# Nine slots of the first three experts: plain loads in place of gathers in a two-stage FFT and expert kernel

## The chip, the cores and the metric

The kernel runs on one core of a Trainium2 chip. The metric is the device time of one execution in microseconds (us); lower is better. The engines are named as the profile names them: PE (TensorE, with PEld for its weight loads), DVE (VectorE), ACT (ScalarE), POOL (GpSimd) and SP (SyncE, which here only issues DMAs). The times shown are those of three runs; one further execution was profiled.

## The reference

The input `x` has 8 batches of 1856 rows of 256 numbers. The real part of its two-dimensional Fourier transform per batch gives 14,848 tokens of 256 features. Each token goes to one of 16 experts (4 groups of 4), and each expert is a two-layer network.

```
X = np.fft.fft(np.fft.fft(x, axis=1), axis=2).real      # 8 x 1856 x 256 -> tokens
g_idx = argmax(tokens @ w_group)                        # group
e_idx = argmax(tokens @ w_expert[g_idx])                # expert in the group
h = relu(token @ w1[g_idx, e_idx])                      # 256 -> 1024
out[token] = g_weight * e_weight * (h @ w2[g_idx, e_idx])  # 1024 -> 256
```

## The kernel before

Phase 1 (`phase1`) goes through the eight batches: it folds the rows, multiplies with cosine and sine tables, picks an expert for each token (`route`) and scatters the tokens, 260 words each, into a table `XS` in DRAM. There each expert owns 122 x 128 rows. A block of 128 rows is a slot, and seven slots of each expert (`NSLOT`) are static, which means that they are always computed. Rows beyond them are handled in overflow slots. The scatters are indirect DMAs on POOL's queue, 14 or 15 per batch. The order of work in phase 1 is written out by hand in the strings `ORDER0` to `ORDER8`.

Phase 2 (`phase2`) is a list of jobs. Jobs 0, 1 and 2 are the first four slots of experts 0, 1 and 2. They are "early": their rows are all there after an early batch, or are left as they were filled. Jobs 3, 4 and 5 are the remaining three static slots of experts 0, 1 and 2 (together the nine slots of the change). From job 6 on, each further expert has a job of four slots, one of three and one overflow slot. A scheduler in the compiler sets the order of the instructions on each engine where the code does not pin it.

A job needs its rows `xg` in SBUF. `turn_steps` makes of each slot a high half (`xh`, an ACT cast) and a low half (`xh`, a DVE subtraction), and a DMA transpose on SP's queue writes both to `xT`. Layer 1 (`layer1`) takes 8 blocks of hidden units, 6 matmuls `ph` each. ACT and DVE then write `hT` from `ph`. There are four `ph` buffers (`UB`), so block 4 waits for the `hT` of block 0. Layer 2 (`layer2`) takes 24 matmuls `py` per slot, an ACT step that writes `y`, and a scatter to `out` on POOL. The weights of each expert come in four parts (`wst`, 512 KB each, on SP's queue).

The rows of a static slot come by an indirect DMA on POOL's queue (`gather`). Its indices `ii` lie outside the table for rows beyond the expert's count, so these rows of the buffer stay as they were. There are eight `xg` buffers (`XGB`), all set to 1 at the beginning. The rows of an early slot come by plain DMAs on SP's queue (`early_load`). For that reason the twelve early slots of `XS` are filled with ones at the beginning, in the first pass over the batches, so that no row of them is undefined.

Of the kernel before, what the change touches and what calls it, by code (L numbers as in the profile page):

```python
# [10 lines left out]
F32 = mybir.dt.float32  # L11
F16 = mybir.dt.float16
I32 = mybir.dt.int32
# [9 lines left out]
P = 128  # L23
# [7 lines left out]
CAP = ROWS * P  # L31
RWID = 260
NSLOT = 7
# [66 lines left out]
def earliest():  # L100

    return {e: n for _, w in waves() for e, _, n in w}
# [156 lines left out]
def bc(ap, axis, n):  # L259

    a = ap.unsqueeze(axis)
    shape = list(a.shape)
    shape[axis] = n
    return a.broadcast_to(shape)


class K:
# [538 lines left out]
    def phase1(self):  # L806
        tc, nc, cp, ps = self.tc, self.nc, self.cp, self.ps
        self.late, rows = ExitStack(), ExitStack()
        xp, ub, rp = (s.enter_context(tc.tile_pool(name=n, bufs=k, side="right"))
                      for s, n, k in ((self.late, "xq", 4), (self.late, "ub", 1), (rows, "row", 1)))  # L810
        with tc.tile_pool(name="ua", bufs=1) as ua, tc.tile_pool(name="fft", bufs=1) as fp:
            self.fp = fp
            self.misc = ps.tile([P, 512], F32, name="misc", tag="misc")
            self.load_small()
            xs = {0: self.load_x(0, xp, 2)}
            self.CS = fp.tile([P, 2, 2, 4, NK], F16, name="CS")
            cs = self.ap["cs"].rearrange("p (t h c k) -> p t h c k", t=2, h=2, c=4)
            for tr in range(2):
                for c in range(4):
                    nc.sync.dma_start(out=self.CS[:, tr, :, c], in_=cs[:, tr, :, c])  # L820
                if tr == 0:
                    nc.sync.dma_start(out=self.c16, in_=self.ap["c16"])
                    xs[1] = self.load_x(1, xp)
            self.rt = self.wp.tile([P, 4096], F32, name="wst")[:, 0:512]
            nc.sync.dma_start(out=self.rt, in_=self.ap["c32"][:, C_RT:])
            nc.sync.dma_start(out=self.c32[:, C_LATE:], in_=self.ap["c32"][:, C_LATE:C_RT])
            self.carry = self.c32[:, C_OFF:C_OFF + NE]
            self.ex = [cp.tile([P, NCM, 2, 5], F32, name=f"ex{i}") for i in range(2)]
            for ex in self.ex:
                nc.gpsimd.memset(ex, 1e-9)  # L830
            whl = self.wpa.tile([P, 2, 4096], F16, name="whl").rearrange("p h n -> p (h n)").bitcast(F32)
            self.rowts = [whl[:, 0:NC * RWID].rearrange("p (n d) -> p n d", d=RWID),
                          rp.tile([P, NCM, RWID], F32, name="row")]
            self.rowt = {}
            for t in self.rowts:
                nc.gpsimd.memset(t[:, :, D + 2:RWID], 0.0)
            for i in range(XGB):
                xg = self.xp2.tile([P, RWID], F32, name="xg")
                nc.gpsimd.memset(xg, 1.0)

            def run(gens, order, rest=True, keep="N"):

                for _ in self.run(gens, order):
                    pass
                for k, g in gens.items():
                    if rest and g and k not in keep:
                        for _ in g:
                            pass

            self.queues = {k: [] for k in "sIidlt"}  # L850
            self.fds, Us = {}, {}
            self.open = self.parts = 0
            self.first = {"G": self.fold(0, xs.pop(0), fp), "H": self.nyquist_in()}
            run(self.first, START, False)
            F, W, X, Z = self.fold(1, xs.pop(1), fp), None, None, None
            for b in range(B):
                g = {"Z": Z, "F": F}
                F = None
                if b + 2 < B:
                    xs[b + 2] = self.load_x(b + 2, xp)  # L860
                    F = self.fold(b + 2, xs.pop(b + 2), fp)
                g["N"] = F
                if b == 0:
                    for e, n in earliest().items():
                        self.Q.dma_start(out=self.XS[e * CAP:e * CAP + n * P].rearrange("(s p) c -> p s c", p=P),
                                         in_=bc(xg[:, :].bitcast(I32), 1, n))
                if b == W0_AT:
                    self.st0 = self.wp.tile([P, 4096], F32, name="wst")
                    for i in range(8):
                        s = slice(i * 512, i * 512 + 512)  # L870
                        self.later("t", lambda s=s: tc.keep_in_program_order(
                            nc.sync.dma_start(out=self.st0[:, s], in_=self.ap["w12"][0, :, s])))
                Us[b] = (ua, ub)[b % 2].tile([P, 2, 2, NK], F16, name="U")
                g["S"] = self.s_stage(b, Us[b])
                g["U"] = self.nyquist_rows(b, Us[b], ub)
                if b == 0:
                    g.update(self.first)
                    g["Y"] = self.first["Y"] = self.nyquist()
                    g["R"] = self.router_weights()
                else:  # L880
                    g.update(self.rows_of(b - 1, Us.pop(b - 1), xp))
                if b == 5:
                    W, X = self.first_weights(), self.first_turn()
                g["W"], g["X"] = W, X
                Z = g["R"] if 0 < b < LASTZ else None
                run(g, {0: ORDER0, 5: ORDER5, 6: ORDER6, 7: ORDER7}.get(b, ORDER),
                    keep="N" + ("R" if Z else "") + ("WX" if b < B - 1 else ""))
            self.last = self.rows_of(B - 1, Us.pop(B - 1), xp)
            rows.close()
# [51 lines left out]
    def early_load(self, e, r, Q):  # L941

        xg = self.xp2.tile([P, RWID], F32, name="xg")
        o = e * CAP + r * P
        self.of_batch(Q.dma_start(out=xg[:, :].bitcast(I32), in_=self.XS[o:o + P, :]).ins, self.early[e, r][0])
        return xg

    def of_batch(self, ins, b):
# [219 lines left out]
    def phase2(self, wp):  # L1168
        tc, nc = self.tc, self.nc
        wpa = self.wpa  # L1170
        with tc.tile_pool(name="h", bufs=2, reuse_waits="tile") as hp, \
# [10 lines left out]
            first = earliest()  # L1182
# [7 lines left out]
            for e in range(len(first), NE):  # L1190
# [3 lines left out]
                o = e - len(first)  # L1194
# [17 lines left out]
            st, ready, infos, xs = {}, {0: self.w0}, {}, {}  # L1212
# [3 lines left out]
            def tail():  # L1216
                if state["tail"]:
                    try:
                        next(state["tail"])
                    except StopIteration:  # L1220
                        state["tail"] = None
                        pool["wo"] = later.enter_context(
                            tc.tile_pool(name="wo", bufs=1, side="right", reuse_waits="tile"))
# [32 lines left out]
            def fetch(n):  # L1256
                if n >= len(jobs):
                    return
                _, kind, slots = jobs[n]
                if kind != "e" and not infos:  # L1260
                    while state["tail"]:
                        tail()
                    infos["s"] = self.static_info()
                    infos["o"] = self.overflow_info()
                if kind == "e":
                    if n >= len(self.x0):
                        xs[n] = [self.early_load(*j, nc.sync) for j in slots], [self.early[j][1] for j in slots]
                else:
                    ii, ge = infos[kind]
                    xs[n] = ([self.gather(self.xp2, ii[:, j:j + 1]) for j in slots],  # L1270
                             [ge[:, j:j + 1] for j in slots])

            def prep(n):
# [13 lines left out]

            pend = None
            fetch(0)
            finish(prep(0))  # L1290
            fetch(1)
            loads()
            for n, (u, kind, slots) in enumerate(jobs):
# [69 lines left out]
```

## Time and profile before

| what | value |
|---|---|
| median of three runs | 862.84 us (862.5 to 863.77) |
| profiled execution, own time | 861.9 us |
| its span, first to last instruction | 860.1 us |
| PE busy | 807.9 us (94%) |
| ACT, DVE, POOL busy | 579.1, 533.5, 385.1 us |
| mean granted TensorE clock | 0.985 of full speed |
| gathers of static slots | 100, 106.8 us of POOL |

The table is read from the busy shares of the page. PE is the engine with the largest share, so a stage in which PE stands still is where time can be gained or lost.

### The profile page before, as it was taken

How to read it: one execution, taken by the hardware profiler on the slowest of the kernel's cores; microseconds unless marked ns; L12 is line 12 of the kernel's file. 1: busy time of each engine (PE TensorE's matmuls, PEld its weight loads, DVE VectorE, ACT ScalarE, POOL GpSimd, SP SyncE). 2: the span in 40 equal slices, each digit the busy share in tenths (PEclk: the TensorE clock that was granted, in tenths of full speed). 3: DMA queues.
4: the chain of work that ended last, by engine and by line, in shares of the span. 5: the costliest groups of instructions: out<-in, count | busy, mean ns of one | idle time of the engine just before them, and what ended most of it. 6: DMA issues, size and time to landing. Idle time of an engine off the chain costs nothing.

```text
span 860.1 us, 17724 instructions
## 1 busy us (share of the span) xinstructions
PE 807.9 (94%) x6375; PEld 578.8 (67%) x6375; DVE 533.5 (62%) x1346; ACT 579.1 (67%) x1190; POOL 385.1 (45%) x372
## 2 busy tenths in 40 slices
PE   2789899969979999999999999999999999999997
PEld 0457666647547767676768686868686868686866
DVE  6499989666736456474838474747475656654440
ACT  2477667776738578595959687777677776866441
POOL 1007777776876425334434343435252526240303
PEclk9999999979989999999999999999999999999999
DMA  9914663585697545465756465757474848261201
GB/s 347 356 65 172 220 229 120 179 241 150 209 295 152 182 149 178 150 172 161 182 163 190 154 190 149 209 133 222 123 231 111 255 87 271 69 170 40 57 10 42
DMA packets 110186, 145.89 MB, mean 170 GB/s; under 512 B 76395, under 2 KB 81799, under 8 KB 108304
## 3 DMA queue, kind: packets, MB, share of 16 engines
q1 hardware_dynamic: 92768, 99.96, 38.9%
q0 software_dynamic: 16896, 44.55, 17.4%
q8 instruction: 51, 0.84, 0.4%
q14 instruction: 39, 0.32, 0.1%
q10 hardware_dynamic: 432, 0.22, 0.1%
HBM read 97.18 MB, written 33.29 MB: 152 GB/s over the span
## 4 chain that ended last, share of the span: by engine, by line
PE 56%; issue 6%; ACT 4%; DMA 4%; DVE 2%; POOL 1%; POOLq 0%; SPq 0%; ACTq 0%; DVEq 0%
PE ph L1129 28%; PE py L1145 28%; DMA xT<-xh 2%; ACT junk L245 2%; ACT whl L245 1%; POOL out L797 1%; DMA wst<-w 1%; ACT hT L1132 1%; DVE hT L1133 1%; DMA xg<-XS,ii_s 1%; DVE whl L245 1%; ACT y L1150 0%; ACT xh L1090 0%; DVE xh L1092 0%; DVE e_v L245 0%
## 5 line engine op out<-in xcount | busy, mean ns | idle before, releaser
L1129 PE MATMUL ph<-xT,whl 128*128 128x512 f16 (+2 forms) x2112 | 355.5, 318 | 13.0 <-DVE hT L1133 6.0
L1145 PE MATMUL py<-whl,hT 128*128 128x256 f16 x2976 | 354.2, 273 | 0.7 <-ACT y L1150 0.5
L1145 PEld LDWEIGHTS <-hT 128*128 128x128 f16 x2976 | 288.5, 98 | 55.7 <-issue 1.2
L1133 DVE SCALAR_TENSOR_TENSOR hT<-ph,hT 128x512 f16<-128x512 f32 (+2 forms) x352 | 179.6, 529 | 151.3 <-ACT hT L1132 149.5
L1129 PEld LDWEIGHTS <-whl 128*128 128x128 f16 x2112 | 182.3, 98 | 133.7 <-issue 16.5
L797 POOL DMA_INDIRECT out<-y,tok x124 | 136.7, 1102 | 267.9 <-ACT y L1150 238.9
L1132 ACT ACTIVATE hT<-ph 128x512 f16<-128x512 f32 (+2 forms) x352 | 157.0, 473 | 64.3 <-PE ph L1129 62.0
L1076 POOL DMA_INDIRECT xg<-XS,ii_s x100 | 106.8, 1068 | 99.0 <-ACT xh L1090 43.7
L245 DVE SCALAR_TENSOR_TENSOR whl<-wst,e_v,whl 128x1024 f16<-128x1024 f32 x112 | 137.8, 1281 | 19.8 <-ACT whl L245 19.6
L245 ACT ACTIVATE whl<-wst,e_v 128x1024 f16<-128x1024 f32 x112 | 120.9, 1139 | 14.5 <-DVE e_v L245 12.8
L245 ACT ACTIVATE junk<-wst 128x1024 bf16<-128x1024 f32 x112 | 119.1, 1063 | 7.7 <-DMA wst<-w 7.7
L1150 ACT ACTIVATE y<-py,cws 128x256 f32<-128x256 f32 x124 | 58.3, 471 | 69.5 <-PE py L1145 64.8
L1092 DVE TENSOR_TENSOR xh<-xg,xh 128x256 f16<-128x256 f32 x112 | 46.5, 419 | 87.3 <-ACT xh L1090 87.2
L245 PE MATMUL pu<-CS,ghl 128*128 128x464 f16 (+3 forms) x384 | 83.9, 369 | 4.6 <-ACT ghl L245 4.6
L797 POOL DMA_INDIRECT XS<-whl,posi x42 | 44.9, 1070 | 74.6 <-ACT row L245 62.3
L1090 ACT CAST xh<-xg 128x256 f16<-128x256 f32 x112 | 42.8, 402 | 50.7 <-DMA xT<-xh 40.4
L245 PEld LDWEIGHTS <-ghl 128*128 128x128 f16 (+1 forms) x384 | 44.3, 119 | 35.9 <-ACT ghl L245 4.9
L797 POOL DMA_INDIRECT XS<-row,posi x45 | 50.2, 1116 | 14.0 <-issue 11.6
L245 PEld LDWEIGHTS <-U 128*128 128x128 f16 x672 | 44.3, 99 | 12.9 <-issue 5.4
L245 PE MATMUL pr<-c,U 128*128 128x256 f16 x336 | 47.6, 279 | 3.4 <-ACT row L245 2.5
L245 DVE TENSOR_TENSOR xq<-xq 128x514 f32<-128x514 f32 x64 | 41.1, 685 | 6.4 <-DMA xq<-xq 6.3
L245 ACT CAST U<-pu 128x464 f16<-128x464 f32 (+3 forms) x64 | 33.2, 549 | 9.2 <-PE pu L245 8.9
(150 smaller groups left out, 429.7 us busy)
## 6 DMA issues: line engine op xcount, KB each, us to landing
wst<-w SPq DMA_DIRECT2D x108, 512.0 KB
xq<-xq SPq DMA_DIRECT2D x14, 1028.0 KB
CS<-cs SPq DMA_DIRECT2D x8, 464.5 KB
xq<-xq SPq DMA_DIRECT2D x4, 514.0 KB
wst<-w SPq DMA_DIRECT2D x8, 256.0 KB
xT<-xh SPq DMA_TRANSPOSE x124
out<-y,tok POOLq DMA_INDIRECT x124, 4.0
xg<-XS,ii_s POOLq DMA_INDIRECT x100, 6.4
```

Of the source, the lines that this page charges most:

```text
L245: return self.tc.keep_in_program_order(f(*args, **kw))
L797: ins = self.nc.gpsimd.indirect_dma_start(out=out, out_offset=bass.IndirectOffsetOnAxis(ap=ap, axis=0), in_=in_, in_offset=None, bounds_ch ...
L1076: self.nc.gpsimd.indirect_dma_start(out=xg[:, :].bitcast(I32), out_offset=None, in_=self.XS[:, :], in_offset=bass.IndirectOffsetOnAxis(ap= ...
L1090: A.copy(xh[:, 0], xg[:, 0:D])
L1092: lo = V.tensor_tensor(out=xh[:, 1], in0=xg[:, 0:D], in1=xh[:, 0], op=ALU.subtract)
L1129: nc.tensor.matmul(ph[:, 0:n * P], lhsT=w[:, wl, o:o + P], rhs=xT[:, xl * 2 + c, :], start=i == 0, stop=i == 5)
L1132: nc.scalar.activation(hT[:, f, 0], ph[:, 0:n * P], AF.Relu)
L1133: nc.vector.scalar_tensor_tensor(out=hT[:, f, 1], in0=ph[:, 0:n * P], scalar=0.0, in1=hT[:, f, 0], op0=ALU.max, op1=ALU.subtract)
L1145: nc.tensor.matmul(py, lhsT=hT[:, f, hl, j * P:(j + 1) * P], rhs=w[:, wl, 2048 + f * D:2048 + (f + 1) * D], start=i == 0, stop=i == 23)
L1150: nc.scalar.activation(y, py, AF.Copy, scale=cw)
```

## The change

`XS` is filled with ones in two steps: the early slots 0 to 3 of experts 0, 1 and 2 in the pass of batch 0, as before, and their slots 4 to 6 in the pass of batch 1. The nine slots are then read with `row_load`, a plain DMA of 128 rows on SP's queue, and no longer with `gather` on POOL's queue.

```diff
-                if b == 0:
+                if b < 2:
                     for e, n in earliest().items():
-                        self.Q.dma_start(out=self.XS[e * CAP:e * CAP + n * P].rearrange("(s p) c -> p s c", p=P),
-                                         in_=bc(xg[:, :].bitcast(I32), 1, n))
+                        r0, r1 = ((0, n), (n, NSLOT))[b]
+                        self.Q.dma_start(out=self.XS[e * CAP + r0 * P:e * CAP + r1 * P].rearrange("(s p) c -> p s c", p=P),
+                                         in_=bc(xg[:, :].bitcast(I32), 1, r1 - r0))
...
+    def row_load(self, j):
+
+        xg = self.xp2.tile([P, RWID], F32, name="xg")
+        o = j // NSLOT * CAP + j % NSLOT * P
+        self.nc.sync.dma_start(out=xg[:, :].bitcast(I32), in_=self.XS[o:o + P, :])
+        return xg
...
-                    xs[n] = ([self.gather(self.xp2, ii[:, j:j + 1]) for j in slots],
+                    xs[n] = ([self.row_load(j) if kind == "s" and j < len(first) * NSLOT else
+                              self.gather(self.xp2, ii[:, j:j + 1]) for j in slots],
                              [ge[:, j:j + 1] for j in slots])
```

On SP's queue, at the end of phase 1, stand the parts of the weights of an overflow slot (four `wst` with an ISA row ahead of each), of expert 3 (the other four `wst`), and the transposes of jobs 3 to 5. Before:

```order
L1026 DMA wst<-w 128x1024
...
L1026 DMA wst<-w 128x1024 x2
L1098 DMA_TRANSPOSE xT<-xh 128x4x128
L1026 DMA wst<-w 128x1024 x2
L1098 DMA_TRANSPOSE xT<-xh 128x4x128 x12
```

And with the change:

```order
L953 DMA xg<-XS 128x260 x8
L1034 ISA
L1034 DMA wst<-w 128x1024
...
L1034 DMA wst<-w 128x1024 x2
L1106 DMA_TRANSPOSE xT<-xh 128x4x128 x3
L953 DMA xg<-XS 128x260
L1034 DMA wst<-w 128x1024 x3
L1106 DMA_TRANSPOSE xT<-xh 128x4x128
```

Eight of the nine row loads now stand ahead of the overflow weights, and five parts of weights stand between them and the first three transposes, those of job 3; before, six stood ahead of the first of these and eight ahead of the other two.

On ACT, in the same stretch, the casts `xh` of jobs 3 and 4 stand between the `y` of job 1 and the `hT` of job 2 (`hT_3269` before, `hT_3260` with the change). Before:

```order
L1150 ACTIVATE y_3414<-py_3389,cws_2949 128x256
L1090 CAST xh_3281<-xg_3000 128x256
L1132 ACTIVATE hT_3269<-ph_3270 128x512
L1132 ACTIVATE hT_3269<-ph_3283 128x512
L1132 ACTIVATE hT_3269<-ph_3295 128x512
L1132 ACTIVATE hT_3269<-ph_3306 128x512
L1090 CAST xh_3304<-xg_3004 128x256
```

And with the change:

```order
L1158 ACTIVATE y_3405<-py_3380,cws_2952 128x256
L1098 CAST xh_3272<-xg_3003 128x256
L1098 CAST xh_3295<-xg_3005 128x256
L1098 CAST xh_3318<-xg_3007 128x256
L1098 CAST xh_3515<-xg_3254 128x256
L1140 ACTIVATE hT_3260<-ph_3261 128x512
L1140 ACTIVATE hT_3260<-ph_3274 128x512
```

One cast stood ahead of the first `hT` of job 2 before, and four stand there now. On PE the order of the same stretch moves too. Before, 27 matmuls `py` stand between the first 24 and the second 24 matmuls `ph` of job 2, and 53 between those and the first `ph` of job 3; with the change it is 38 and 14, and the other 28 stand among the `ph` of job 3. On POOL nine gathers fall away.

## Rows read from the trace of the kernel before

**Rows 1.** Page, part 1: busy us, share of span, instructions.

```profile
PE 807.9 (94%) x6375; PEld 578.8 (67%) x6375; DVE 533.5 (62%) x1346; ACT 579.1 (67%) x1190; POOL 385.1 (45%) x372
```

**Rows 2.** Timeline of PE, 231 to 263 us: start, us, what, idle before.

```profile
231.40 5.35 PE L1129 MATMUL ph<-xT,whl 128*128 128x512 f16 x24 [1.11 <-ACT whl L245]
236.59 3.11 PE L1145 MATMUL py<-whl,hT 128*128 128x256 f16 x27
245.38 8.20 PE L1129 MATMUL ph<-xT,whl 128*128 128x512 f16 x24 [5.68 <-DVE hT L1133]
253.42 5.95 PE L1145 MATMUL py<-whl,hT 128*128 128x256 f16 x53
259.20 4.06 PE L1129 MATMUL ph<-xT,whl 128*128 128x384 f16 x24
```

**Rows 3.** Waits, 236 to 262 us: total us, times, longest.

```profile
ACT xh L1090 <- DMA xg<-XS,ii_s: 9.4, 3, 8.5
```

**Rows 4.** Timeline of ACT, 234 to 262 us.

```profile
243.70 0.40 ACT L1090 CAST xh<-xg 128x256 f16<-128x256 f32 x1 [8.52 <-DMA xg<-XS,ii_s]
244.01 2.05 ACT L1132 ACTIVATE hT<-ph 128x512 f16<-128x512 f32 x4
...
256.57 0.41 ACT L1090 CAST xh<-xg 128x256 f16<-128x256 f32 x1 [0.18 <-DMA xT<-xh]
...
258.34 0.41 ACT L1090 CAST xh<-xg 128x256 f16<-128x256 f32 x1 [1.36 <-DMA xT<-xh]
```

**Rows 5.** Timeline of POOL, 231 to 239 us.

```profile
231.53 1.98 POOL L797 DMA_INDIRECT XS<-xq,posi  x1 [0.30 <-issue]
...
237.42 1.04 POOL L1076 DMA_INDIRECT xg<-XS,ii_s  x1 [0.30 <-issue]
```

**Rows 6.** Chain that ended last, 200 to 310 and 590 us: start, us.

```profile
237.42 6.26 DMA xg<-XS,ii_s
...
590.42 3.55 DMA xT<-xh
```

**Rows 7.** Waits of SP's queue, 200 to 300 us.

```profile
SPq L1026 <- DMA XS<-xq,posi: 4.3, 2, 3.4
```

**Rows 8.** Timeline of SP's queue: start and length of issue.

```profile
167.61 5.46 SPq L245 DMA_DIRECT2D xg<-XS  x8
...
206.94 1.81 SPq L945 DMA_DIRECT2D xg<-XS  x4
...
236.49 5.14 SPq L1026 DMA_DIRECT2D wst<-w  x6
...
247.48 2.57 SPq L1098 DMA_TRANSPOSE xT<-xh  x2
```

**Rows 9.** Timeline of ACT, 171 us: the first cast behind the eight loads.

```profile
171.40 0.41 ACT L245 CAST xh<-xg 128x256 f16<-128x256 f32 x1 [0.33 <-DMA xg<-XS]
```

**Rows 10.** DMA queues, 240 to 245 us, then 245 to 250: packets, MB, share.

```profile
q1 hardware_dynamic: 440, 1.61, 81.4%
...
q1 hardware_dynamic: 830, 1.16, 74.6%
```

**Rows 11.** Timeline of PE, phase 1: two earlier pauses.

```profile
41.32 0.81 PE L245 MATMUL pu<-U,c 127*127 127x464 f16 x2 [1.96 <-ACT U L245]
...
107.32 0.97 PE L245 MATMUL pr<-c,U 128*128 128x256 f16 x6 [2.23 <-ACT row L245]
```

**Rows 12.** Busy by window: PE, PEld, DVE, ACT, POOL, PEclk, DMA share, GB/s.

```profile
40.00:44.00 4.00, 2.58 (x30) 2.08 (x30) 1.26 (x5) 3.08 (x6) 0.00 (x0) 1.00 0.72 282
44.00:58.00 14.00, 13.65 (x114) 9.26 (x113) 13.93 (x30) 10.55 (x25) 0.00 (x0) 1.00 0.01 2
...
108.00:112.00 4.00, 4.00 (x28) 2.28 (x27) 3.65 (x10) 2.04 (x7) 3.08 (x4) 0.59 0.60 216
...
245.00:252.00 7.00, 6.62 (x18) 2.40 (x18) 4.79 (x12) 3.62 (x9) 5.19 (x6) 0.56 1.06 346
```

**Rows 13.** Timeline of POOL: the first scatter to the table.

```profile
65.53 1.26 POOL L797 DMA_INDIRECT XS<-whl,posi  x1 [62.25 <-ACT row L245]
```

## The prediction, made before the run

> **What bounds the kernel now.** I read the busy shares first. PE is busy for 94% of the span [rows 1], so I looked for the places where it is not, and for one that the nine gathers touch. In the timeline of PE there is such a place at the passage from phase 1 to phase 2 [rows 2]: PE ends its 27 `py` at 239.70 (236.59 + 3.11) and starts the second half of job 2's layer 1 only at 245.38, after a pause of 5.68 us. Those 24 `ph` then take 8.20 us, where the first 24 took 5.35. [...] So this place costs 5.68 + (8.20 - 5.35) = 8.53 us.
>
> The cause of the pause stands two engines away. PE waits for DVE's `hT`, DVE for ACT, and ACT sits 8.52 us in front of a cast of job 3's first slot whose gather has not landed [rows 3, 4]. Behind this cast stand the four `hT` of job 2 that PE needs. The gather is issued at 237.42 and lands 6.26 us later [rows 5, 6]. It can't be much earlier on any queue: the last scatter to the table is issued at 231.53 [rows 5], and SP's queue waits 3.4 us for it [rows 7] and issues its next DMA at 236.49 [rows 8]. After this place I see no pause that matters until job 3 begins at 259.20 [rows 2]. The transposes of job 3 are only just in time for it, though. The two of 247.48 [rows 8] are seen landed when they give back buffers to casts at 256.57 and 258.34, each ended by a DMA of `xT` [rows 4], and the second is the last that job 3 needs. It was 9.6 us under way (258.34 less 248.77, half of 2.57 us after 247.48).
>
> **What the change adds at the beginning.** Three fills of 384 x 1040 bytes, 1.2 MB, go out behind the load of batch 3. Between 44 and 58 us the DMA engines are used to 0.01 [rows 12], and the first scatter, which has to wait for the fills, starts at 65.53 and waits for ACT until then [rows 13]. I cost them at nothing; this quiet stretch hides them. Without it they would take 1.2 MB at the 0.28 MB per us seen between 40 and 44 us [rows 12], 4.3 us.
>
> **What it removes.** Nine gathers at about 1.04 us and 0.30 us of idle each on POOL [rows 5], 12 us. POOL is not what PE waits for, so this is worth nothing by itself.
>
> **What it moves: the loads.** Eight row loads now start on SP when the last scatter has landed, at 236.4. One takes 0.45 us to issue (1.81 / 4 [rows 8]), so they go out between 236.4 and 240.0. ACT has four casts ahead of the first `hT`, so the fourth load counts; it is issued at 237.75. How long a plain load takes to land I bound from above by the first of eight, issued at 167.61 and seen landed at a cast at 171.40 [rows 8, 9]: 3.8 us. The gather's 6.26 us [rows 6] lies further off, with 3 MB of weights beside it on the DMA engines. From below I have the issue itself, 0.45. I take 3.0, nearer to the plain load, since no weights run beside these loads: the fourth cast starts at 240.8. From a cast to PE's next `ph` it took 1.68 us (243.70 to 245.38). So PE goes on at 242.5. It has 11 more `py` before that, at 0.112 us (5.95 / 53), and ends them at 240.9. The pause shrinks from 5.7 to 1.6 us. A pause of 1.96 us left the clock at 1.00, one of 2.23 was followed by 0.59 over 4 us [rows 11, 12]. I take no loss of clock here. PE then does 24 `ph` in 5.35 us and 14 `py` in 1.6, and is ready for job 3 at about 249.4.
>
> **What is late next.** Job 3's transposes are on SP's queue behind the eight loads and five parts of weights. Eight loads of 133,120 bytes and five parts of 524,288 make 3.69 MB. SP's queue moved 0.32 MB per us between 240 and 245 us and 0.23 in the next 5 us [rows 10]. I take 0.30, near the first, because the gathers that ran beside it come later now: 12.3 us from 237.2, when the first data can flow, so the weights are through at 249.5. For the three transposes I add 2.5 us (two that followed each other landed 1.77 apart [rows 4]; the first comes right behind the weights). Job 3's `xT` is there at 252.0. At 0.40 MB per us, which would be queue and neighbours together, it would be 248.9, in time; at 0.23, with 3.5 us for the transposes, 256.7.
>
> [...]
>
> **The sum.** Before, job 3 starts at 259.20. Now it starts at 252.0, with 28 `py` still to be done: 28 x 0.112 = 3.1. The gain is 259.2 - 3.1 - 252.0 = 4.1 us. PE has then paused from 249.4 to 252.0, 2.6 us. By the two earlier pauses [rows 11] this is long enough for a stretch at the lower clock; 4 us at 0.59 [rows 12] cost 1.65. The net gain is 2.4 us. Counted the other way: before 8.53, now 1.6 + 2.6 + 1.65 = 5.9; the small rest is in the rounding of the blocks. From there to the end PE is the bound and I let the gain run through. The profiled execution of 861.9 becomes 859.5; it stands 0.9 below the median, and 862.84 becomes **860.4 us**.
>
> **Rivals.** Changes of less than 0.2% (1.7 us) can't be told from none.
>
> First, the transposes are in time. SP's line moves at 0.38 MB per us or more (3.69 MB by 246.9), PE finds `xT` ready at 249.4 and no clock is lost. The gain is 259.2 - 3.1 - 249.4 = 6.7: 856.1 us. For it speaks that no gathers compete at first, against it that the same transposes were only just in time before. Chance 0.19.
>
> Second, the change does not do what it says: the loads land no faster than gathers, 6.26 us after their issue. The fourth is there at 244.0, PE goes on at 245.7 as before, its clock falls as before, and job 3 starts at 245.7 + 8.2 + 1.6 = 255.5, by then with its `xT`. The gain is 0.6: 862.2 us. For it speaks that both wait for the same last scatter, against it the 3.8 us of the plain load. Chance 0.15.
>
> Third, slower: the line on SP's queue moves at 0.23 MB per us and job 3 starts at 256.7, with the pause of 7.3 us followed by a low clock like that of before, 3.1 us (0.44 of 7 us [rows 12]). That is 259.2 - 3.1 - 256.7 - 3.1 = -3.7: 866.5 us. It decides from a start of job 3 at 256.1, where nothing is gained even at full clock, or at 254.5 with one short stretch of low clock. For it speaks the rate of 245 to 250 us; against it, that three transposes and more scatters were part of that stretch. Chance 0.12.
>
> My forecast has 0.54. Of this I put 0.38 above 1.7 us of gain and 0.16 below, since a low clock that lasts like the one of before (3.1 in place of 1.65) leaves 1.0. So faster 0.38 + 0.19 = 0.57, same 0.16 + 0.15 = 0.31, slower 0.12. The range goes from 856.3, just short of the first rival's best, to 863.3, where the forecast ends with a start of job 3 at 253.5 and a low clock of 3.1 (259.2 - 3.1 - 253.5 - 3.1 = -0.5); it leaves out most of the third rival and little else.
>
> **What would show it.** In the profile after: row loads on SP from about 236.4; the fourth cast near 240.8; a pause of PE of 1 to 2 us at 241, and the next 24 `ph` in about 5.3 us. Then a second pause before the first `ph` of 384 columns, ended by a DMA of `xT`, near 252. If this second pause is missing, the first rival holds. If the first `hT` of job 2 still comes at 244, the second holds. I'm wrong as a whole if the order of jobs 4 to 6, which moves too, opens a pause further on, or if the fills delay the first scatter.

## The result, and the profile after

| | us |
|---|---|
| before, median of 17 runs | 863.70 (860.5 to 867.73) |
| with the change, median of 17 runs | 869.65 (866.2 to 874.22) |
| ratio, 95% interval | 1.0067 [1.0051, 1.0083] |
| predicted | 860.4, range 856.3 to 863.3 |
| profiled execution with the change | 871.9, span 870.1 |

The change makes the kernel slower by 0.67%, 5.9 us. The prediction's sign was wrong, and the time lies outside its range.

Timeline of PE with the change, the place of [rows 2]:

```profile
237.10 4.31 PE L1153 MATMUL py<-whl,hT 128*128 128x256 f16 x38
243.70 5.34 PE L1137 MATMUL ph<-xT,whl 128*128 128x512 f16 x24 [2.29 <-DVE hT L1141]
248.88 1.69 PE L1153 MATMUL py<-whl,hT 128*128 128x256 f16 x14
257.93 5.41 PE L1137 MATMUL ph<-xT,whl 128*128 128x384 f16 x18 [7.36 <-DMA xT<-xh]
```

The first pause is 2.29 us in place of 5.68, and the 24 `ph` behind it take 5.34 in place of 8.20. A second pause has come, 7.36 us ahead of job 3, ended by a transpose. The timelines of ACT and of SP's queue show why:

```profile
239.26 0.41 ACT L1098 CAST xh<-xg 128x256 f16<-128x256 f32 x1 [3.57 <-DMA xg<-XS]
239.93 0.41 ACT L1098 CAST xh<-xg 128x256 f16<-128x256 f32 x1 [0.26 <-DMA xg<-XS]
241.71 0.72 ACT L1098 CAST xh<-xg 128x256 f16<-128x256 f32 x2 [1.38 <-DMA xg<-XS]
242.34 2.05 ACT L1140 ACTIVATE hT<-ph 128x512 f16<-128x512 f32 x4
...
256.54 0.40 ACT L1098 CAST xh<-xg 128x256 f16<-128x256 f32 x1 [9.45 <-DMA xT<-xh]
```

```profile
236.99 3.77 SPq L953 DMA_DIRECT2D xg<-XS  x8
241.23 2.84 SPq L1034 DMA_DIRECT2D wst<-w  x5
244.54 6.41 SPq L1106 DMA_TRANSPOSE xT<-xh  x3
251.00 0.57 SPq L953 DMA_DIRECT2D xg<-XS  x1
```

The fourth cast is at 242.0 (the second of the two from 241.71), and the four `hT` that PE needs follow at once. ACT waits for rows for 5.2 us in all (3.57 + 0.26 + 1.38), in place of 8.52 in [rows 4]. But the first transpose of job 3, issued at 244.54, gives its buffer back only at 256.54. The windows (columns as in [rows 12]) show the price in clock and what the DMA engines did meanwhile:

```profile
240.00:245.00 5.00, 2.71 (x20) 1.70 (x19) 3.54 (x12) 3.38 (x8) 0.18 (x1) 1.00 0.95 310
...
250.00:255.00 5.00, 0.57 (x6) 0.27 (x3) 0.00 (x0) 0.00 (x0) 0.00 (x0) 1.00 1.26 213
255.00:258.00 3.00, 0.07 (x1) 0.10 (x2) 0.49 (x2) 0.78 (x3) 0.00 (x0) 0.64 1.02 202
258.00:263.00 5.00, 5.00 (x17) 2.36 (x18) 3.58 (x10) 4.24 (x10) 3.87 (x4) 0.53 1.09 376
```

After the 2.29 us the granted clock is 1.00; after the 7.36 it is 0.53 over 5 us, and 18 `ph` take 5.41 us. In hold0_c below they take 3.08; before, 24 of them took 4.06 [rows 2] with a granted clock of 1.00 from 259.2 to 263.2 us.

The second loss is at the very end. PE's last row in the timeline, of before and with the change:

```profile
851.78 2.35 PE L1145 MATMUL py<-whl,hT 128*128 128x256 f16 x20
```

```profile
851.77 9.01 PE L1153 MATMUL py<-whl,hT 128*128 128x256 f16 x81
```

POOL's drains in the view of the kernel's last source line (ns, shortest, middle and longest of three, then first and last start in us), of before and with the change:

```profile
L1359 POOLq DRAIN  x3: 40/103/802, 858.5 to 859.8; - x3
```

```profile
L1368 POOLq DRAIN  x3: 40/103/4069, 865.2 to 869.8; - x3
```

Before, PE ends at 854.13 and the span at 860.1, 6.0 us later. With the change it is 860.78 and 870.1, 9.3 us. One drain of POOL takes 4.07 us in place of 0.80.

Nine of the runs below (fills_only, loads_pool, hold0, before_hold0, hold0_b, loads_pool_b, after_b, after_nine and hold2_nine) fell to chips on which the kernel before took 952 to 964 us in place of 863 to 865, with idle time of PE and ACT that is put down to their own instructions, so their ratios, from 0.987 to 1.003, are not used, only rows of their traces.

Two figures return in all of the runs. The **stretch** is the time from PE's first `ph` of job 2 to its first `ph` of job 10; in every kernel the same 384 `ph` and 552 `py` lie in it. The **end** is the time from PE's last matmul to the end of the span. Before they are 135.0 and 6.0 us, with the change 139.0 and 9.3. Each is read from one profiled execution, and the stretch scatters: kernels with the order of before gave 133.6 (loads_pool_c) to 137.9 (before_seven). The end does not, it is within 0.1 us for each program.

### The profile page after: what moved, and what is told of

It reads as the page before. It is cut to its first block, busy times and chain, and to the rows that moved or that the text cites. A ratio compares the mean times of both kernels' runs of the same rounds, so it can differ in the third digit from the quotient of the medians.

```text
span 870.1 us, 17716 instructions
## 1 busy us (share of the span) xinstructions
PE 805.8 (93%) x6375; PEld 578.2 (66%) x6375; DVE 533.8 (61%) x1346; ACT 579.5 (67%) x1190; POOL 379.0 (44%) x363
## 4 chain that ended last, share of the span: by engine, by line
PE 61%; issue 5%; DMA 3%; POOL 1%; ACT 1%; DVE 1%; SPq 0%; POOLq 0%; ACTq 0%
PE ph L1137 31%; PE py L1153 30%; DMA xT<-xh 2%; POOL out L797 1%; DMA XS<-xq,posi 1%; DMA xg<-XS 0%; ACT whl L245 0%; DVE hT L1141 0%; SPq L1106 0%; DVE xh L1100 0%; ACT hT L1140 0%; ACT xh L1098 0%; POOL XS L797 0%; ACT y L1158 0%; SPq L953 0%
## 5 line engine op out<-in xcount | busy, mean ns | idle before, releaser
L797 POOL DMA_INDIRECT out<-y,tok x124 | 138.7, 1119 | 270.7 <-ACT y L1158 225.9
L1084 POOL DMA_INDIRECT xg<-XS,ii_s x91 | 97.7, 1073 | 109.6 <-ACT hT L1140 34.1
L797 POOL DMA_INDIRECT XS<-row,posi x45 | 50.7, 1126 | 13.9 <-issue 11.9
```

What stands on the lines that cost most here:

```text
L797: ins = self.nc.gpsimd.indirect_dma_start(out=out, out_offset=bass.IndirectOffsetOnAxis(ap=ap, axis=0), in_=in_, in_offset=None, bounds_ch ...
L1084: self.nc.gpsimd.indirect_dma_start(out=xg[:, :].bitcast(I32), out_offset=None, in_=self.XS[:, :], in_offset=bass.IndirectOffsetOnAxis(ap= ...
```

## The experiments

Theory A: the loss at the place is the wait for job 3's transposes, which stand on SP's queue behind eight row loads and five parts of weights. Rivals: B, the fills cost it; C, the new order on PE and ACT does it by itself; D, the row loads slow the DMA engines as a whole.

**The fills alone.** The second pass of fills is kept, the nine slots are gathered.

```diff
-                    xs[n] = ([self.row_load(j) if kind == "s" and j < len(first) * NSLOT else
+                    xs[n] = ([self.row_load(j) if False else
```

> Only the second pass of fills is kept; the nine slots are gathered as before, and the order of phase 2 on every engine is that of before. Theory A (the loss comes from job 3's transposes, which stand on SP's line behind eight row loads and five parts of weights): the fills are hidden in the quiet stretch at 44 to 58 us, ratio to before within 0.998 to 1.002, first scatter at about 65.5 us. Theory B (the fills cost the time): ratio 1.004 to 1.007 and a later first scatter.

> The second pass of fills alone, gathers kept, the order of phase 2 that of before. Theory A: ratio 0.998 to 1.002, first scatter at about 65.5 us. Theory B (the fills cost the time): 1.004 to 1.007.

The second run gave 0.9997 [0.9975, 1.002], a stretch of 135.2 and an end of 6.0. The first scatter in the timeline of POOL is not later than in [rows 13]:

```profile
65.08 1.26 POOL L797 DMA_INDIRECT XS<-whl,posi  x1 [61.81 <-ACT row L245]
```

B falls as the cause.

**The plain loads on POOL's queue.** The order on all engines is that of before; only the kind of transfer differs (and the fills).

```diff
-        self.nc.sync.dma_start(out=xg[:, :].bitcast(I32), in_=self.XS[o:o + P, :])
+        self.nc.gpsimd.dma_start(out=xg[:, :].bitcast(I32), in_=self.XS[o:o + P, :])
```

> The nine plain loads are issued on POOL's queue in place of the gathers; the order on SP, PE, ACT and POOL is exactly that of before, so that only the kind of transfer differs (and the fills). Theory A: nothing is added to SP's line, so nothing is lost; if a plain load lands about 3 us after its issue in place of 6.26, the pause of 5.7 us shrinks to 2.5 to 3.5 and the ratio is 0.996 to 1.000 (job 3's transposes, still behind eight parts of weights, may take the rest back in a second pause). Theory D (the row loads themselves are slow or burden the DMA engines): a pause of 5.5 us or more, or a second pause of 4 us or more ahead of job 3, and a ratio of 1.003 or more.

> The run loads_pool again for the same reason: plain loads on POOL's queue, the order of before on every engine. Theory A: ratio 0.996 to 1.000, first pause 2.5 to 3.5 us in place of 5.7, nothing lost ahead of job 3 beyond what the pause gives. Theory D: first pause 5.5 us or more, or a second of 4 us or more, ratio 1.003 or more.

> Plain loads on POOL's queue, the order of before on every engine, so that only the kind of transfer differs from the run above. Theory A: nothing is added to SP's line; the first pause shrinks from 5.7 to 2.5 to 3.5 us if plain loads land sooner than gathers there too, job 3's transposes stay behind eight parts of weights as before, and the ratio is 0.996 to 1.001. Theory D: 1.003 or more.

The last run gave 1.0016 [0.9993, 1.0039], just above A's range, stretch 133.6, end 6.0. Timelines of SP's queue, of ACT and of PE:

```profile
235.50 5.94 SPq L1034 DMA_DIRECT2D wst<-w  x6
```

```profile
244.91 0.40 ACT L1098 CAST xh<-xg 128x256 f16<-128x256 f32 x1 [8.36 <-DMA xg<-XS]
```

```profile
246.59 7.02 PE L1137 MATMUL ph<-xT,whl 128*128 128x512 f16 x24 [5.52 <-DVE hT L1141]
```

The pause did not shrink to 2.5 to 3.5 us: it is 5.52, as with gathers. In the first two runs PE came so late that there was no first pause to read. The first load of the last one was issued at 237.26 and seen landed at 244.91, 7.65 us, with six parts of weights beside it. So the plain kind is not what made the loads fast in the change. D wanted a ratio of 1.003 or more, which the interval just reaches and the stretch doesn't bear out; the next run settles it.

**The weights held behind job 3's transposes**, in the change (hold0) and in the kernel before (before_hold0). The dependency (`NoSync`, `SCHED_ONLY`) is there for the order in which SP issues; the timeline of hold0_c has the eight parts at 247.51, behind the three transposes of 242.20.

```diff
-            Q.dma_start(out=xT[:, :, j * P:(j + 1) * P], in_=xh, transpose=True)
+            self.turned = Q.dma_start(out=xT[:, :, j * P:(j + 1) * P], in_=xh, transpose=True).ins.name
...
+                if n == 3:
+                    self.t3 = self.turned
...
+            self.wn = getattr(self, 'wn', 0) + (hasattr(self, 't3') and not pin)
+            if 0 < self.wn <= 8:
+                self.tc.add_manual_dep(ins.ins, self.t3, mybir.DependencyInfo(
+                    mybir.DependencyClass.NoSync, mybir.DependencyReason.SCHED_ONLY), reason="behind job 3's")
```

> The change, with the eight parts of weights of the overflow slot and of expert 3 held behind the transposes of job 3 on SP. PE's order has 38, 10 py where the change has 38, 14. Theory A: job 3's xT is there by 249, the second pause (7.36 us with the change) falls below 1 us, the first stays at 2 to 2.5, the granted clock stays up, and the ratio to before is 0.992 to 0.996 (some 855 to 860 us where before is 862 to 864). Theory C (the new order on PE and ACT, four casts ahead of job 2's hT and few py ahead of job 3, is the cause): the second pause stays at 4 us or more, ratio 1.003 or more. Theory D (row loads slow the DMA engines as a whole): transposes land after 253, ratio 1.000 or more.

> The run hold0 again, since in the runs of that call every kernel, the one before too, took some 960 us and PE, ACT and POOL stood still for their own instructions (idle put down to issue) at the very place in question, so that neither pause could be read. Where before takes about 863 us: theory A: job 3's xT is there by 249, the second pause (7.36 us with the change) falls below 1 us, the first stays at 2 to 2.5, ratio 0.992 to 0.996. Theory C (the order on PE and ACT): second pause 4 us or more, ratio 1.003 or more. Theory D (row loads slow the DMA engines as a whole): transposes land after 253, ratio 1.000 or more.

> The change with all eight parts of weights held behind job 3's transposes, now that before takes about 865 us again. Theory A (the wait for job 3's xT behind the weights is the loss): transposes land 2.3 to 3.5 us after their issue, the pause ahead of job 3 is 3 us or less in place of 7.36, and the ratio is 0.994 to 1.000, at least 0.006 below that of the change (1.0067). Theory C (the order on PE and ACT is the cause): this order is like that of the change, so 1.004 or more. Theory D (row loads slow all of the DMA engines): transposes 7 us or more under way, 1.004 or more.

hold0_c gave 1.0025 [1.0006, 1.0045], stretch 135.1, end 9.3. Timelines of SP's queue and PE:

```profile
242.20 3.85 SPq L1110 DMA_TRANSPOSE xT<-xh  x3
246.09 0.58 SPq L953 DMA_DIRECT2D xg<-XS  x1
247.51 4.23 SPq L1034 DMA_DIRECT2D wst<-w  x8
252.38 9.29 SPq L1110 DMA_TRANSPOSE xT<-xh  x3
```

```profile
242.63 5.34 PE L1141 MATMUL ph<-xT,whl 128*128 128x512 f16 x24 [1.29 <-DVE hT L1145]
247.81 1.25 PE L1157 MATMUL py<-whl,hT 128*128 128x256 f16 x10
249.01 3.08 PE L1141 MATMUL ph<-xT,whl 128*128 128x384 f16 x18
...
265.91 1.12 PE L1141 MATMUL ph<-xT,whl 128*128 128x384 f16 x3 [2.90 <-DVE xh L1104]
```

Job 3 starts at 249.01 without a pause, though four casts stand ahead of `hT` and only 10 `py` ahead of job 3. C falls as the cause of the 7.36 us, D with it (the same row loads stand on SP's queue), and A holds there. But the eight parts now stand ahead of job 4's transposes, and the wait comes back at 265.91: ACT waited 5.38 us for a transpose, and the clock is 0.57 over the next 8 us.

```profile
265.04 0.40 ACT L1102 CAST xh<-xg 128x256 f16<-128x256 f32 x1 [5.38 <-DMA xT<-xh]
```

```profile
265.00:273.00 8.00, 6.88 (x33) 4.39 (x34) 7.12 (x21) 7.58 (x14) 5.05 (x5) 0.57 0.61 126
```

The stretch is 3.9 us shorter than the change's and no shorter than before's. The end is that of the change, so the two ratios can be set side by side: 1.0067 and 1.0025, 0.0042 or 3.6 us apart, with intervals that don't meet. That is what the hold gives back, net of the wait at job 4. A's range, 0.994 to 1.000, was missed, by the longer end and by the wait that came back. In hold0 and hold0_b the transposes took 2.3 to 2.6 us too; PE came late there, so that the missing pause ahead of job 3 says nothing.

> The kernel before (gathers, no new fills) with the same weights held behind the transposes of job 3; the order on PE becomes like that of the run above (38, 10 py) and four casts stand ahead of job 2's hT. Theory A: the hold alone gives nothing, since four gathered slots are now waited for ahead of the first hT: the first pause grows from 5.7 to 7 to 9 us with a low clock after it, and no second pause; ratio 0.999 to 1.004. Theory C (order): a ratio of 1.005 or more, like the change. If the ratio is 0.996 or less, the weights ahead of the transposes were a loss before too and the plain loads are not needed for the gain.

> The kernel before with its weights held behind job 3's transposes: gathers, and the order on PE and ACT that the change has (38, 10 py; four casts ahead of job 2's hT). Theory A: no wait for xT, but four gathers are waited for ahead of the first hT, so the first pause grows from 5.7 to 7 to 9 us; ratio 0.999 to 1.004. Theory C: 1.005 or more.

before_hold0_c gave 1.0043 [1.0023, 1.0063], stretch 138.3, end 6.0. Timelines of ACT and PE:

```profile
240.30 0.40 ACT L1094 CAST xh<-xg 128x256 f16<-128x256 f32 x1 [5.08 <-DMA xg<-XS,ii_s]
...
245.92 0.41 ACT L1094 CAST xh<-xg 128x256 f16<-128x256 f32 x1 [2.37 <-DMA xg<-XS,ii_s]
```

```profile
247.60 6.95 PE L1133 MATMUL ph<-xT,whl 128*128 128x512 f16 x24 [6.67 <-DVE hT L1137]
```

The ratio is just above A's range and its interval reaches C's 1.005, the pause (6.67 us) is just below A's 7 to 9. So the order may cost some of this time: the four gathers that are waited for ahead of `hT` are part of it. With no weights beside it, a gather issued at 237.44 is seen landed at 240.30, 2.9 us, against 6.26 in [rows 6]: not much slower than a plain load of the change (issued at 236.99, cast at 239.26, 2.3 us). So what the change gained at the first pause, it gained by putting the rows ahead of the weights, and by issuing four of them in 1.9 us (half of 3.77) where POOL needs 1.3 us for each gather (1.04 and 0.30 of idle [rows 5]).

**Two and three parts of weights ahead, and one idle DMA.** hold2 and hold3 hold all parts from the third or fourth on (`2 < self.wn`, `3 < self.wn`). The runs named _one add an idle DMA on POOL (one whose data nothing uses), for the end (below).

> The change with two parts of weights ahead of job 3's transposes on SP in place of five (six are held behind them). Theory A is about how long a transpose is under way behind weights: with five parts ahead it took 7.2 to 10.7 us from issue to landing, with none 2.3 to 2.4. With two parts it should take 3 to 5.5 us, and the pause ahead of job 3 should be 1 us or less. Time: where before takes about 863 us, ratio 0.992 to 0.997; where it takes about 955, ratio 0.99 to 1.002, not to be told from before. If the rows before the weights or the gathers beside (theory D), not the weights, hold the transposes up, they take 7 us or more here too.

> The change with two parts of weights ahead of job 3's transposes (six held behind them) and the one idle DMA on POOL; the order is that of the run hold2, whose ratio was 1.0001 with an end of 9.4 us. Theory T: the end falls to 6.0 us and the ratio to 0.994 to 0.999. Rival: 9.4 us and 0.998 to 1.002. Theory A: pause ahead of job 3 about 2.8 us as in hold2, no first pause.

> The same with three parts ahead of job 3's transposes and five behind; the order moves a little with it (four transposes of jobs 4 and 5 stand behind the five). Theory A: a transpose is under way 4 to 6.5 us, between the 3.5 of two parts and the 8.3 to 10.7 of five; the pause ahead of job 3 is 2 to 4.5 us; with an end of 6.0 us the ratio is 0.994 to 1.000. If transposes take 8 us or more here, it is not the weights ahead of them that count.

They gave 1.0001 [0.9979, 1.0024], 1.002 [1.0, 1.004] and 1.004 [1.0022, 1.0058], with stretches of 132.2, 135.2 and 135.1 and ends of 9.4. The table has the time of job 3's three transposes, read from the traces: from the start of the issue to the last of the landing events that the trace records for it (16 for each of the three, before and with the change). Ahead are the bytes of SP's line that its packets had not yet moved when the first of the three was issued.

| run | parts of weights ahead | MB ahead | us, one by one |
|---|---|---|---|
| hold0_c | 0 | 0.1 | 2.5, 2.4, 2.4 |
| before_hold0_c (gathers beside) | 0 | 0 | 4.6, 5.1, 4.4 |
| the kernel before (gathers beside) | 6, 8, 8 | 1.07 | 5.6, 9.0, 9.4 |
| hold2 | 2 | 0.75 | 3.8, 3.6, 3.8 |
| hold2_one | 2 | 0.83 | 4.8, 4.2, 3.7 |
| hold3_one | 3 | 1.38 | 6.5, 6.1, 5.3 |
| the change | 5 | 2.26 | 11.9, 11.1, 8.5 |
| after_one | 5 | 2.33 | 11.9, 11.3, 10.5 |

This is A's curve: the more is ahead, the longer a transpose is under way, 2.4 us with nothing and near 4, 6 and 11 us with two, three and five parts. Weights are not all of it: with gathers beside them and no weights ahead the transposes took 4.4 to 5.1 us. In the kernel before they were nearly as slow as in the change; but the last landed at 258.24, while PE was at its 53 `py` until 259.2, so that nothing waited. Timelines of PE and ACT in hold2:

```profile
241.09 5.34 PE L1141 MATMUL ph<-xT,whl 128*128 128x512 f16 x24
...
250.30 4.76 PE L1141 MATMUL ph<-xT,whl 128*128 128x384 f16 x18 [2.78 <-DVE hT L1145]
```

```profile
246.00 0.40 ACT L1102 CAST xh<-xg 128x256 f16<-128x256 f32 x1 [3.88 <-issue]
247.19 0.41 ACT L1102 CAST xh<-xg 128x256 f16<-128x256 f32 x1 [0.78 <-DMA xT<-xh]
248.63 0.40 ACT L1102 CAST xh<-xg 128x256 f16<-128x256 f32 x1 [1.03 <-DMA xT<-xh]
248.94 2.05 ACT L1144 ACTIVATE hT<-ph 128x512 f16<-128x512 f32 x4
```

The first pause is gone and the stretch is 2.8 us shorter than before. Of the second pause 2.78 us are left: three casts that need buffers from the transposes stand on ACT ahead of job 2's last four `hT`. Here the order on ACT (C) does cost, though not the 7.36.

That the first pause is gone can't be put down to the order. hold2_one has the same order, a first pause of 2.02 us and a stretch of 135.2, no shorter than before. In this one execution of hold2 the row loads were early: the first was issued 2.45 us after job 2's first `ph` (231.75), in hold2_one 4.59 us after it (232.79). Timelines of SP's queue in hold2 and hold2_one:

```profile
234.20 4.27 SPq L953 DMA_DIRECT2D xg<-XS  x8
```

```profile
237.38 3.79 SPq L954 DMA_DIRECT2D xg<-XS  x8
```

What the orders are worth is better read from the ratios, since the end is the same in all of them, some 3.4 us longer than before. Less these 3.4 us, hold2 is 3.3 us faster than before, hold2_one 1.7, hold0_c 1.2, hold3_one the same, and after_one and the change are 1.8 and 2.4 slower, each give or take 2 us. In total none is faster than before; for hold2, A had wanted 0.992 to 0.997 and a second pause of 1 us or less.

**The end.** The change with one idle DMA on POOL, and the kernel before with seven:

```diff
+        nc.gpsimd.dma_start(out=self.cp.tile([P, 8], F32, name="pad"), in_=self.ap["c32"][:, 0:8])
```

> The change plus one idle DMA of 4 KB on POOL's queue at the beginning, so that POOL has 344 DMAs and the two of the overflow loop use the first two of its eight semaphores, as before. The order on all engines is that of the change. Theory T (the end is 3.3 us longer because those two DMAs fall on the last and the first semaphore): the time from PE's last matmul to the end is 6.0 us in place of 9.3, ratio 1.001 to 1.005 in place of 1.0067. Rival (the row loads on SP make the end longer): 9.3 us, ratio 1.005 to 1.008. The place before job 3 stays as with the change: a pause of 6 to 8 us for xT.

> The kernel before plus seven idle DMAs of 4 KB on POOL's queue at the beginning: 359, so that the overflow loop's two DMAs fall on the last and the first semaphore, as with the change. Nothing else differs. Theory T: the end is 9.3 us in place of 6.0, ratio 1.002 to 1.006 (3.3 us are 0.0038). Rival (row loads): 6.0 us, ratio 0.998 to 1.002.

after_one gave 1.006 [1.0039, 1.0081], stretch 139.9, end 9.4, with 8.80 us of pause ahead of job 3: both losses of the change are there again. before_seven gave 1.0033 [1.0018, 1.0049]; its end is only 6.7, its stretch 137.9, with a pause of 0.84 us ahead of job 3 and a single one of 1.71 near 340 us that no other run of this order shows. The ratio is in T's range, but the end makes only 0.7 of its 2.9 us; where the rest comes from stays open. The longest drain of each (after_one, then before_seven):

```profile
L1369 POOLq DRAIN  x3: 51/103/4154, 865.1 to 869.8; - x3
```

```profile
L1361 POOLq DRAIN  x3: 51/103/1377, 866.3 to 868.2; - x3
```

My theory T, that the two semaphores of the overflow loop do it, falls both ways by the ends: 9.4 where it wanted 6.0, and 6.7 where it wanted 9.3. The drains go by POOL's number of DMAs: 343 in the change, hold0 and hold2, 4.07; 344, 4.15; 352 in before and its variants, 0.80 to 0.81; 359, 1.38. That is 0.08 us for each DMA more, and a fall somewhere between 344 and 352. The last two runs fill 343 up to 352:

```diff
+                if 20 <= n < 29:
+                    nc.gpsimd.dma_start(out=self.cp.tile([P, 1], F32, name=f"pad{n}"), in_=cw[0])
```

> The change plus nine idle DMAs of 512 bytes on POOL's queue, one in each of jobs 20 to 28, so that POOL has 352 DMAs as before; the order of everything else is that of the change. Theory N (the last drain of POOL goes by the number of DMAs on its queue, 0.08 us for each since some point between 344 and 352): drain 0.8 us, 6.0 us from PE's last matmul to the end, ratio 1.002 to 1.005 in place of 1.0067. Rival (the row loads on SP lengthen the end): 9.3 us and 1.005 to 1.008. Theory A: the place is unchanged, a pause of 7 to 9 us ahead of job 3.

> The run hold2 (the change with only two parts of weights ahead of job 3's transposes; ratio 1.0001, end 9.4 us) plus the same nine idle DMAs. Theory N: drain 0.8 us, end 6.0 us, ratio 0.995 to 0.999. Rival: 9.4 us, 0.998 to 1.002. Theory A: pauses of 2 to 3 us at most around job 3, transposes 3.2 to 4.6 us under way.

The drain of after_nine:

```profile
L1370 POOLq DRAIN  x3: 45/103/811, 940.4 to 941.7; - x3
```

Both kernels, with the row loads on SP, end 6.0 us after PE's last matmul. hold0, which fell to such a chip as these two and has 343 DMAs, ends 9.3 us after it. Theory N holds: the number of POOL's DMAs does it, not the row loads as such. The two ratios, 0.994 [0.9895, 0.9985] and 0.9899 [0.9848, 0.995], are of those not used: the fills alone, which made no difference in fills_only_c, had 0.9873 [0.976, 0.9986] there. The pause of 7 to 9 us ahead of job 3 that was expected of after_nine is not there; the next part says why.

**The change where PE is late.**

> The change itself, once more, to see what it does where the kernel before takes some 960 us because the engines often stand still for their own instructions. Theory A, if before takes about 863 us in this call: ratio 1.005 to 1.008, second pause about 7 us. If before takes about 960: PE reaches job 3's first ph later relative to the row loads (a stall on ACT ahead of job 1's last weights delays PE but not SP), so the transposes have more time, the second pause is below 4 us, and the ratio is 0.995 to 1.005. Theory C (the order on PE and ACT): a ratio of 1.005 or more in both cases.

The ratio is 0.999 [0.9928, 1.0052], of those not used. In the timeline of PE job 2 starts late, for instructions:

```profile
297.25 6.71 PE L1137 MATMUL ph<-xT,whl 128*128 128x512 f16 x24 [4.96 <-issue]
...
318.03 5.92 PE L1137 MATMUL ph<-xT,whl 128*128 128x384 f16 x18 [3.21 <-DVE xh L1100]
```

The same program pauses 3.21 us ahead of job 3 in place of 7.36, because the row loads did not wait for PE. In four executions with five parts ahead, the pause follows the time from job 2's first `ph` to the issue of the first row load:

| run | first row load after job 2's first `ph`, us | pause ahead of job 3, us |
|---|---|---|
| after_one | 5.2 | 8.80 |
| the change | 5.1 | 7.36 |
| after_b | 0.4 | 3.21 |
| after_nine | -2.5 | none |

That is A again: the pause is what SP's line lacks in lead over PE.

## Why the prediction was wrong, point by point

- **The fills cost nothing: right** (0.9997; first scatter at 65.08).
- **The loads and the first pause: right.** Row loads from 236.99 (236.4 forecast), fourth cast at 242.0 (240.8), PE on at 243.70 (242.5), pause 2.29 us (1.6) and no clock lost. The fourth load landed 3.7 us after its issue (3.0). That no weights ran beside the loads was the right reason for a short landing; that they are plain loads was not. A plain load beside weights took 7.65 us (loads_pool_c), a gather without them 2.9 (before_hold0_c).
- **"Job 3's `xT` is there at 252.0": the step that failed.** It was there at 257.8, by the last landing event of the third transpose, and PE began job 3 at 257.93. Both terms were too small. The first data of the line moved at 237.95, not 237.2, and the last packet of the five parts ended at 252.9, not 249.5: 3.69 MB in 14.9 us, 0.25 MB per us where I took 0.30 (the row beside it, [rows 10], had 0.23). From there the transposes took 4.9 us more, not 2.5. I had priced them from two that landed 1.77 us apart; here the second and third landed 1.1 and 0.2 us after the one before, and it was the first that came late, 3.6 us after the weights' last packet. Gathers ran beside it (POOL's queue moved 0.39 MB between 250 and 255 us) and may be a part of that; no run separates it. So `xT` came only 0.4 us earlier than before (258.24), and PE had 28 `py` less to do until then. So the third rival's mechanism came true, its start of 256.7 outdone by 1.2 us, and I had given it 0.12.
- **The line on SP's queue: right, but an estimate.** The 252.0 counts job 3's transposes as waiting for all that stands ahead of them on SP's queue. No row read before the run shows that; it was my estimate. The trace of the change shows it there: the 17 DMAs issued on SP's queue from 236.99 to 251.00 landed in the order of issue, by the last landing event of each, the fifth part of weights at 254.93, the first transpose at 256.44. That transpose took 11.9 us with five parts ahead of it; in hold0_c, with none, it took 2.5.
- **The clock: right in kind.** The 24 `ph` of 8.20 us before ran at a granted clock of 0.56 from 245 to 252 us [rows 12]. With the change the first 18 `ph` of job 3 took, after the long pause, 2.3 us longer than in hold0_c (5.41 for 3.08), at a granted clock of 0.56 from 257.93 to 263.34; the forecast had 1.65, the third rival 3.1.
- **"From there to the end PE is the bound and I let the gain run through": the second step that failed.** Nine DMAs fewer on POOL cost 3.3 us in its last drain. I had called the nine gathers less worth nothing; nothing in the trace of before shows this cost, since its drain took 0.80.
- **The range.** Its lower end of 856.3 lies above the first rival's 856.1, so it left out more than "most of the third rival and little else".
- **The sum.** With the measured start of job 3 and the measured clock loss the prediction's own sum comes out near the stretch: 259.2 - 3.1 - 257.9 - 2.3 = -4.1 us. Stretch +4.0 (after_one +4.9) and end +3.3 make 7.3 to 8.2 us; the ratio's interval is 4.4 to 7.2. The profiled execution of after lies 2.25 above its median and that of before 1.8 below, so single executions scatter by more than the rest. In the profiled execution one more pause of 2.10 us at 533.76 is part of its 871.9; after_one, of the same order, has none there.
- Left open: what in the drain follows the count of DMAs, where between 344 and 352 it falls, and whether the order of hold2 with 352 DMAs is faster than before where that takes 863 us. By the ratios of hold2 and hold2_one less their longer end it would be, by an estimated 1.7 to 3.3 us; it was not measured there.

## What to carry to other kernels

When a load is moved to a queue that also carries weights and transposes, list what stands in that queue ahead of the next transfer that an engine needs, and price the whole line at the slowest rate seen near it; what is gained at one wait can be lost at the next one behind it, as it was here. Whether rows come by gather or by plain load mattered less here than whether weights were ahead of them or beside them. Compare the time from the last matmul to the end of the span too: a change in the number of POOL's DMAs moved it by 3.3 us without any row of work.

## What the runs showed of the hardware that was not expected

- POOL's last drain went by the number of DMAs that its queue had had, in steps of 0.08 us, and fell back: 4.07 us at 343, 4.15 at 344, 0.80 at 352, 1.38 at 359.
- Busy DMA engines did not always move much here. In the 5 us from 250 in the change their busy share was 1.26 (0.72 for SP's queue and 0.54 for POOL's) at 213 GB/s, with the last of the five parts of weights (to 252.9), transposes and gathers side by side, where row loads and weights from 240 made 310 GB/s at 0.95.
- The length of the pause just before did not by itself decide the clock. After 2.29 us (the change), 2.32 (hold3_one) and 2.51 (after_one) the 24 `ph` took 5.34, in the change at a granted clock of 1.00 (243.70 to 249.00); after 2.02 us in hold2_one they took 7.03, at a granted clock of 0.76 over 7 us:

```profile
244.31 7.03 PE L1142 MATMUL ph<-xT,whl 128*128 128x512 f16 x24 [2.02 <-DVE hT L1146]
```
